# An attention kernel: one exponential over two PSUM banks, row maxima and projections on three shared banks

## The chip, the cores and the metric

The kernel runs on one core of a Trainium2 chip. The core's engines each work through their own list of instructions: TensorE (PE, matrix products into PSUM), VectorE (DVE), ScalarE (ACT, exponentials and copies), GpSimd (POOL) and SyncE (SP, which issues DMAs here). They wait for each other through semaphores. PSUM has eight banks of 128 partitions by 512 fp32 values. The metric is the device time of one execution in microseconds; the median of three runs counts.

## What is computed

Two attention layers run over 2,048 positions with 32 heads of 16 dimensions; their outputs are put side by side. Half A is softmax attention, half B a linear attention with softmax feature maps:

```python
# A
q, k, v = split(x @ wqkv)                       # 32 heads x 2048 x 16 each
p = softmax(einsum("bhqd,bhkd->bhqk", q, k) * 16 ** -0.5)
a = einsum("bhqk,bhkd->bhqd", p, v) merged @ wo
# B
pq, pk = q @ w_phi, k @ w_phi                   # per head, 16 x 16
phi = concat([softmax(p_), softmax(-p_)])       # for q and for k
o = (phi_q @ (phi_k.T @ v)) / (phi_q @ sum(phi_k) + 1e-6)
b = o merged @ wo
out = concat([a, b], axis=-1)                   # 2048 x 1024, bf16
```

Half A dominates: 32 x 2048 x 2048 scores are computed twice, once for the row maxima and once, transposed, for the exponentials.

## The kernel before

The program is planned in Python. `_Plan.op` appends an instruction to an engine's list and works out which semaphores it has to wait for from the tokens in `deps`. Each engine then runs its list strictly in the order in which the planner emitted it, so the order of emission is the schedule.

The work of half A is cut into 32 units. A unit `u` is a group `g` of four heads (their dimensions lie on partitions 0, 32, 64 and 96 of `QT` and `KT`) and a chunk `c` of 512 queries. The main loop (L916 on) counts slots `tau`; a unit has 32 slots (`NQ`), so there are 1,024 slots with maxima (`total_q1`).

In each slot the loop emits, in this order:

- `emit_m1(tau)`: the first product, two matmuls (L723), 128 queries by 512 keys for two of the four heads, each into a bank of its own. The heads alternate by slot (`half`), and with them the banks: 0 and 1, or 2 and 3. The matmuls wait for the reduction two slots back (`r1.get(q1 - 2)`). Each unit makes 64 such maxima tiles.
- `emit_m2` for two blocks of the unit that started 43 slots earlier (`LAG`): the second product (L771), 128 keys by 512 queries, scores transposed, with the row maxima subtracted through two extra rows of `QT`. It uses the other two heads' row quarters than the first product of the same slot. Its banks come from a free list, `ring_free`, which starts as banks 4, 5 and 6.
- `emit_exp` for each of the two blocks: one ACT instruction (L782) per bank, into a slot of the 16-deep buffer `pT`. The bank goes back to the free list.
- calls that fall due in this slot (`later`): POOL, ACT and DVE steps of half B (among them two DVE reductions into `mB`, L462 and L464), and the normalisation of a finished unit.
- every second slot `emit_pv`: four matmuls (L796) that sum P.V over keys into bank 7.
- `bg_step`: one piece of a background job, four matmuls as a rule (projections, half B's products, output projection). A job takes the first bank of the free list and gives it back when ACT has been told to copy it out. In 237 slots the trace has a piece of a job; two kinds hold their bank over several slots (half B's key-value products for four, the output projection for two).
- `emit_fill`: matmuls on zeros (L823), so that each slot has at least two groups of four (`NCOL`) beside the two products. They go into bank 7 while P.V is open, or else into the first free bank.
- `emit_r1(tau)`: one DVE reduction (L735) over the two banks of the first product, into `part`.

When a unit's 64 maxima are there, `emit_mchain` reduces `part` to `mrow` (L744), POOL splits the values into two bf16 parts, and DMAs on SP put them into `QT`. After the last unit, `emit_last` normalises it and finishes the output projection of the last four tiles: `emit_acc` has summed seven of the eight groups before (28 matmuls, L874), three tiles early into banks 1 to 3 and one at the end.

The parts that carry the order around the change:

```python
deps = [qt_ready[(g, c)], kt_ready[(g, kc)], r1.get(q1 - 2)]   # emit_m1
bank = ring_free.pop(0)                                        # emit_m2
ring_free.append(bank)                                         # emit_exp
running.append([list(j[2]), j[3], bank, bank_reader.get(bank), j[4]])   # bg_step: a job starts
ring_free.append(r[2])                                         # bg_step: after its last piece
```

Of the kernel before, what the change touches and what calls it, by code (L numbers as in the profile page):

```python
# [6 lines left out]
ALU = mybir.AluOpType  # L7
# [87 lines left out]
def bass_concat_heads__softmax_full_mha__linear_kernel_hedgehog__prompt_kernel(  # L95
# [24 lines left out]
    with contextlib.ExitStack() as es:  # L120
        block = es.enter_context(nc.Block())

        def sb(name, shape, dt):
            return es.enter_context(nc.sbuf_tensor(name, shape, dt))
# [37 lines left out]
        Yd = sb("Yd", [128, 2, 512], F32)  # L162
        lr = sb("lr", [32, 2, 64], F32)
        OA = sb("OA", [128, 2, 512], BF)
        part = sb("part", [128, 2, 4, 4, NKC], F32)
        mrow = sb("mrow", [128, 2, 16], F32)
        trow = sb("trow", [128, 2, 16], F32)
        BD = sb("BD", [128, 4, 128], BF)
# [95 lines left out]
        def later(slot, fn):  # L264
            calls.setdefault(slot, []).append(fn)
# [442 lines left out]
        def decode_q1(q1):  # L708
            u = q1 // NQ
            j = q1 % NQ  # L710
            if u == 0:
                return u, (j // 2) % 4, j // 8, j % 2
            return u, j // (2 * NKC), (j // 2) % NKC, j % 2

        def emit_m1(q1):
            u, qt, kc, half = decode_q1(q1)
            g, c = units[u]
            q0 = c * 512 + qt * 128
            deps = [qt_ready[(g, c)], kt_ready[(g, kc)], r1.get(q1 - 2)]
            tok = None  # L720
            for i in range(2):
                r = 2 * half + i
                tok = P.op("pe", lambda e, r=r: e.matmul(  # L723
                    PS[:, r, :], QT[32 * r:32 * r + 32, g, q0:q0 + 128],
                    KT[32 * r:32 * r + 32, g, kc * 512:(kc + 1) * 512],
                    start=True, stop=True, tile_position=(32 * r, 0)), deps, signal=(i == 1))
                deps = []
            m1[q1] = tok

        def emit_r1(q1):  # L730
            u, qt, kc, half = decode_q1(q1)
            deps = [m1[q1]]
            if q1 % NQ == 0 and u >= 2:
                deps.append(rm_t[u - 2])
            r1[q1] = P.op("dve", lambda e: e.tensor_reduce(  # L735
                part[:, u % 2, 2 * half:2 * half + 2, qt, kc], PS[:, 2 * half:2 * half + 2, :],
                AX.X, ALU.max), deps)

        def emit_mchain(u):
            ub = u % 2  # L740
            deps = [r1[q] for q in range(u * NQ, (u + 1) * NQ)]
            if u >= 2:
                deps.append(lo_t[u - 2])
            rm_t[u] = P.op("dve", lambda e: e.tensor_reduce(  # L744
                mrow[:, ub, :], part[:, ub].rearrange("p a b c -> p (a b) c"), AX.X, ALU.max), deps)
            hi_v = stage[:, ub, 0:16]
            lo_v = stage[:, ub, 16:32]
            hi = P.op("pool", lambda e: e.tensor_scalar(hi_v, mrow[:, ub, :], -1.0, None, ALU.mult),  # L748
                      [rm_t[u], t_stage0, mt_t.get(u - 2)])
            tt = P.op("pool", lambda e: e.tensor_tensor(trow[:, ub, :], mrow[:, ub, :], hi_v, ALU.add), [hi])  # L750
            lo_t[u] = P.op("pool", lambda e: e.tensor_scalar(lo_v, trow[:, ub, :], -1.0, None, ALU.mult), [tt])
            g, c = units[u]
            mt_t[u] = P.dma("sp", d_mt[ub], lambda e: e.dma_start_transpose(mcols[:, ub, :], stage[:, ub, :]),
                            [lo_t[u], mr_t.get(u - 2)])
            for hl in range(2):
                mr_t[u] = P.dma("sp", d_mr[ub], lambda e, hl=hl: e.dma_start(
                    QT[16 + hl:128:32, g, c * 512:(c + 1) * 512], mcols[16 * hl:16 * hl + 16, ub, :]), [mt_t[u]])
# [8 lines left out]
        def emit_m2(B):  # L766
            u, kt, r = block_info(B)
            g, c = units[u]
            bank = ring_free.pop(0)
            bank_of[B] = bank  # L770
            m2_t[B] = P.op("pe", lambda e: e.matmul(  # L771
                PS[:, bank, :], KT[32 * r:32 * r + 32, g, kt * 128:(kt + 1) * 128],
                QT[32 * r:32 * r + 32, g, c * 512:(c + 1) * 512],
                start=True, stop=True, tile_position=(32 * r, 0)),
                [bank_reader.get(bank), mr_t[u], kt_ready[(g, kt // 4)]])
            if B % 2 == 1:
                last_m2[u] = m2_t[B]

        def emit_exp(B):
            slot = B % RING  # L780
            bank = bank_of[B]
            exp_t[B] = P.op("act", lambda e: e.activation(  # L782
                pT[:, slot, :], PS[:, bank, :], ACT.Exp, scale=0.25), [m2_t[B], slot_reader.get(slot)])
            bank_reader[bank] = exp_t[B]
            ring_free.append(bank)

        def emit_pv(u, kt):
            g, c = units[u]
            Bs = [u * NB + 4 * kt + j for j in range(4)]
            deps = [exp_t[B] for B in Bs] + [vp_ready[kt], t_vp1]  # L790
            if kt == 0 and u >= 1:
                deps.append(xev_t[u - 1])
            tok = None
            for B in Bs:
                r = block_info(B)[2]
                tok = P.op("pe", lambda e, B=B, r=r: e.matmul(  # L796
                    PVB[32 * r:32 * r + 17, :], VP[:, kt, 4 * g + r, :], pT[:, B % RING, :],
                    start=(kt == 0), stop=(kt == NKT - 1), tile_position=(0, 32 * r)),
                    deps, signal=(B == Bs[-1]))
                deps = []  # L800
            if u == NU - 1:
                for B in Bs:
                    r = block_info(B)[2]
                    tok = P.op("pe", lambda e, B=B, r=r: e.matmul(  # L804
                        PS[32 * r:32 * r + 32, 0, :], ones_t[:, 0:32], pT[:, B % RING, :],
                        start=(kt == 0), stop=(kt == NKT - 1), tile_position=(0, 32 * r)),
                        [r1[total_q1 - 2]] if kt == 0 else [], signal=(B == Bs[-1]))
            for B in Bs:
                slot_reader[B % RING] = tok
            pv_t[(u, kt)] = tok  # L810
            pv_open[0] = (kt != NKT - 1)

        def emit_fill(ngroups):
            if pv_open[0]:
                bank, dep = 7, None
            elif ring_free:
                bank = ring_free[0]
                dep = bank_reader.get(bank)
            else:
                return  # L820
            for d in range(ngroups):
                for cq in range(4):
                    P.op("pe", lambda e, cq=cq: e.matmul(  # L823
                        PS[32 * cq:32 * cq + 17, bank, :], ones_t[:, 0:17], zmv[:, :],
                        start=(bank != 7), stop=(bank != 7), tile_position=(0, 32 * cq)),
                        [t_zmv, t_ones, dep] if (d == 0 and cq == 0) else [], signal=False)
# [26 lines left out]
        def emit_mul(u, tau):  # L853
            g, c = units[u]
            ub = u % 2
            for half in range(2):
                sl = slice(256 * half, 256 * half + 256)
                lo = c * 512 + 256 * half
                mul_t[u] = P.op("pool", lambda e, sl=sl, lo=lo: e.tensor_tensor(  # L859
                    QT[:, g, lo:lo + 256], X[:, ub, sl], Yd[:, ub, sl], ALU.mult),  # L860
                    [sh_t[u], xev_t[u], last_m2[u]])
            if g == NG - 2 and c == NQC - 1:
                for k in range(3):
                    later(tau + 4 + 2 * k, lambda k=k: emit_acc(k, k + 1, [mul_t[u], r1[total_q1 - 1], t_wo]))
            if g == NG - 1:
                for k in range(4):
                    add_job(tau + 4 + 4 * k, *oproj_job(4 * c + k))
# [11 lines left out]
        def emit_last():  # L879
            u = NU - 1  # L880
            g, c = units[u]
            done = pv_t[(u, NKT - 1)]
            bank = ring_free.pop(0)
            emit_acc(3, bank, [bank_reader.get(bank)])
            ln, ex, ml = {}, {}, {}
            for half in range(2):
                sl = slice(256 * half, 256 * half + 256)
                ln[half] = P.op("act", lambda e, sl=sl: e.activation(Yd[:, 1, sl], PS[:, 0, sl], ACT.Ln),
                                [done, mul_t[u - 2]])
            for half in range(2):  # L890
                sl = slice(256 * half, 256 * half + 256)
# [24 lines left out]
        while tau <= max(pv_in_slot) or jobs or running or calls:  # L916
# [3 lines left out]
            blocks = [2 * Pg, 2 * Pg + 1] if 0 <= Pg < total_q1 else []  # L920
            for B in blocks:
                emit_m2(B)
            for B in blocks:
                emit_exp(B)
            for fn in calls.pop(tau, []):
                fn()
            ncol = 0
# [12 lines left out]
            ncol += bg_step(tau)  # L940
            if ncol < NCOL:
                emit_fill(NCOL - ncol)
            if tau < total_q1:
                emit_r1(tau)
            for u in rm_in_slot.get(tau, []):
                emit_mchain(u)
            tau += 1
# [55 lines left out]
```

## Time and profile before

| | |
|---|---|
| timed runs | 1344.26, 1341.41, 1335.71 us; median 1341.41 |
| profiled execution, its own time (span) | 3156.6 us; no other time is recorded for it |
| DVE busy | 1304.1 us, of which L735 1255.2 (1,024 x 1.226) |
| ACT busy | 1296.2 us, of which L782 1111.5 (2,048 exponentials) |
| POOL busy | 307.0 us |
| PE busy | 3152.2 us in 12,226 matmuls |
| granted TensorE clock | 1.000 throughout |

The profiled execution is one run under the hardware profiler. A busy time is the sum over an engine's instructions, overlaps counted once; a group's line gives source line, engine, operation, what is written from what, the shapes and the count, then busy time and the mean length of one instruction, then the engine's idle time just before them and what ended it. In the timeline the first number is the start in us, the second the length of the merged row, `x8` the number of instructions in it, and the square bracket the idle time before it and what ended it. Matmul ends in it are modelled; the distance from one start to the next is the safer reading. The profiled execution took more than twice as long as the timed runs.

### The profile page before, as it was taken

The numbers are of one execution on the slowest core, as the hardware profiler recorded it, in microseconds if no ns is written. First come the engines' busy times: TensorE is split into PE (matmuls) and PEld (weight loads), VectorE is DVE, ScalarE is ACT, GpSimd is POOL, SyncE is SP. The second block draws the span as 40 slices with busy tenths as digits, with TensorE's granted clock in tenths as the row PEclk, the third lists the DMA queues.
The fourth block names the chain that finished last, engine by engine and source line by source line (L and its number), as shares of the span: only waits on it lengthen the run. The fifth ranks groups of instructions, "written<-read, shape, count | busy, mean of one in ns | idle before, by whom it ended". The sixth has DMA issues, their size and how long they took to land.

```text
span 3156.6 us, 29062 instructions
## 1 busy us (share of the span) xinstructions
PE 3152.2 (100%) x12226; PEld 362.2 (11%) x12226; DVE 1304.1 (41%) x1130; ACT 1296.2 (41%) x2479; POOL 307.0 (10%) x423
## 2 busy tenths in 40 slices
PE   9999999999999999999999999999999999999999
PEld 1111001111111111110011111111111111111111
DVE  1222223444444544544454435444454444445410
ACT  0001223444444444444444435444444444444442
POOL 1000000000011111111111101111111111111100
DMA  2000001000000000000000000000000000100000
GB/s 53 0 0 24 0 11 18 8 2 3 2 2 3 3 6 6 3 3 3 3 3 3 3 8 7 11 11 10 13 10 11 10 16 11 13 10 10 11 5 7
DMA packets 68939, 26.66 MB, mean 8 GB/s; under 512 B 59656, under 2 KB 66824, under 8 KB 68808
## 3 DMA queue, kind: packets, MB, share of 16 engines
q1 hardware_dynamic: 67464, 23.49, 5.4%
q8 instruction: 96, 1.57, 0.2%
q10 hardware_dynamic: 1344, 1.31, 0.1%
q14 instruction: 35, 0.29, 0.0%
HBM read 3.16 MB, written 4.19 MB: 2 GB/s over the span
## 4 chain that ended last, share of the span: by engine, by line
PE 99%; issue 0%; ACT 0%; POOL 0%; DVE 0%; POOLq 0%
PE PS L823 35%; PE PS L723 28%; PE PS L796 11%; PE PS L333 8%; PE PS L452 3%; PE PS L321 3%; PE PS L661 3%; PE PS L528 2%; PE PS L634 2%; PE PS L771 2%; PE PS L369 1%; PE PS L874 1%; PE PS L804 1%; PE PS L589 0%; PE PS L541 0%
## 5 line engine op out<-in xcount | busy, mean ns | idle before, releaser
L735 DVE TENSOR_REDUCE part<-PS 128x2 f32<-128x1024 f32 x1024 | 1255.2, 1226 | 1676.9 <-PE PS L723 1007.5
L782 ACT ACTIVATE pT<-PS 128x512 bf16<-128x512 f32 x2048 | 1111.5, 594 | 1262.1 <-PE PS L771 663.9
L823 PE MATMUL PS<-zmv,ones_t 128*17 128x512 bf16 x5004 | 1217.8, 973 | 0.3 <-ACT pT L782 0.3
L723 PE MATMUL PS<-KT,QT 32*128 32x512 bf16 x2048 | 959.5, 931 | 0.8 <-DVE QT L341 0.8
L771 PE MATMUL PS<-QT,KT 32*128 32x512 bf16 x2048 | 932.2, 902 | 0.0
L796 PE MATMUL PS<-pT,VP 128*17 128x512 bf16 x2048 | 457.2, 782 | 0.0
L723 PEld LDWEIGHTS PS<-KT,QT 32*128 32x128 bf16 x2048 | 111.0, 101 | 1580.8 <-DVE part L735 1102.9
L333 PE MATMUL PS<-xAT,WKp 128*128 128x512 bf16 x128 | 151.8, 1446 | 0.0
L823 PEld LDWEIGHTS PS<-zmv,ones_t 128*17 128x17 bf16 x5004 | 88.9, 88 | 315.1 <-issue 298.6
L771 PEld LDWEIGHTS PS<-QT,KT 32*128 32x128 bf16 x2048 | 111.1, 101 | 64.9 <-ACT pT L782 51.5
L333 PE MATMUL PS<-xAT,WQp 128*128 128x512 bf16 x128 | 116.5, 1122 | 0.0
L748 POOL TENSOR_SCALAR stage<-mrow 128x16 bf16<-128x16 f32 x32 | 8.1, 253 | 1070.4 <-DVE mrow L744 1070.4
L452 PE MATMUL PS<-WKp,xBT 128*128 128x512 bf16 x128 | 106.8, 1051 | 0.0
L345 ACT ACTIVATE KT<-PS,bias_k 128x512 bf16<-128x512 f32 x32 | 22.0, 687 | 194.9 <-PE PS L333 194.9
L507 POOL TENSOR_TENSOR wA<-eB,rB 128x1024 bf16<-128x1024 bf16 x32 | 61.7, 1929 | 398.1 <-ACT rB L501 398.1
L796 PEld LDWEIGHTS PS<-pT,VP 128*17 128x17 bf16 x2048 | 49.6, 87 | 378.0 <-issue 356.3
L321 PE MATMUL PS<-wA,xAT 128*128 128x512 bf16 x64 | 84.3, 1598 | 0.0
L859 POOL TENSOR_TENSOR QT<-X,Yd 128x256 bf16<-128x256 f32 x62 | 43.6, 725 | 400.6 <-DMA Yd<-Yd 400.4
L661 PE MATMUL PS<-WOp,QT 128*128 128x512 bf16 x96 | 80.8, 1063 | 0.0
L486 POOL TENSOR_TENSOR sB<-eB 128x512 f32<-128x512 bf16 x32 | 36.9, 1154 | 374.5 <-ACT eB L479 374.5
L471 POOL TENSOR_TENSOR uB<-pB,mB 128x512 f32<-128x512 f32 x32 | 33.9, 1058 | 395.9 <-DVE mB L462 395.9
L309 ACT ACTIVATE QT<-PS 128x512 bf16<-128x512 f32 x31 | 18.5, 597 | 93.7 <-PE PS L333 93.7
(78 smaller groups left out, 713.8 us busy)
## 6 DMA issues: line engine op xcount, KB each, us to landing
Yd<-Yd SPq DMA_DIRECT2D x124, 32.0 KB, 3.2
out_dram<-xAT SPq DMA_DIRECT2D x16, 128.0 KB, 1.7
out_dram<-OA SPq DMA_DIRECT2D x12, 128.0 KB, 1.7
wA<-in_A_wqkv_dram ACTq DMA_DIRECT2D x2, 512.0 KB, 5.0
QT<-mcols SPq DMA_DIRECT2D x64, 4.0 KB
wA<-in_A_wqkv_dram SPq DMA_DIRECT2D x1, 512.0 KB, 4.3
WOp<-in_A_wo_dram SPq DMA_DIRECT2D x4, 128.0 KB, 4.4
BD<-in_B_w_phi_dram SPq DMA_DIRECT2D x32, 0.5 KB, 1.6
```

Source lines behind the costliest of these rows:

```text
L321: piece = mm_piece(4, lambda e, b, ct: e.matmul(PS[:, b, :], xAT[:, ct, kt * 128:(kt + 1) * 128], wA[:, ct, 1024:1536], start=(ct == 0), s ...
L333: piece = mm_piece(4, lambda e, b, ct: e.matmul(PS[:, b, :], wpad[:, ct, g, :], xAT[:, ct, c * 512:(c + 1) * 512], start=(ct == 0), stop=( ...
L452: add_job(slot, [mm_piece(4, lambda e, b, ct: e.matmul(PS[:, b, :], xBT[:, ct, st * 128:(st + 1) * 128], Wf[:, x, ct, :], start=(ct == 0), ...
L528: piece = mm_piece(4, lambda e, b, ct: e.matmul(PS[:, b, :], xBT[:, ct, st * 128:(st + 1) * 128], wA[:, ct, 0:512], start=(ct == 0), stop= ...
L634: piece = mm_piece(4, lambda e, b, t: e.matmul(PS[:, b, :], oTB[:, i, t, :], woB[:, t, :], start=(t == 0), stop=(t == 3)), lambda: [cx["ot ...
L661: return mm_piece(4, lambda e, b, i: e.matmul(PS[:, b, :], QT[:, 4 * p + i, st * 128:(st + 1) * 128], WOp[:, 4 * p + i, :], start=(p == 0 ...
L723: tok = P.op("pe", lambda e, r=r: e.matmul(PS[:, r, :], QT[32 * r:32 * r + 32, g, q0:q0 + 128], KT[32 * r:32 * r + 32, g, kc * 512:(kc + 1 ...
L735: r1[q1] = P.op("dve", lambda e: e.tensor_reduce(part[:, u % 2, 2 * half:2 * half + 2, qt, kc], PS[:, 2 * half:2 * half + 2, :], AX.X, ALU ...
L771: m2_t[B] = P.op("pe", lambda e: e.matmul(PS[:, bank, :], KT[32 * r:32 * r + 32, g, kt * 128:(kt + 1) * 128], QT[32 * r:32 * r + 32, g, c ...
L782: exp_t[B] = P.op("act", lambda e: e.activation(pT[:, slot, :], PS[:, bank, :], ACT.Exp, scale=0.25), [m2_t[B], slot_reader.get(slot)])
L796: tok = P.op("pe", lambda e, B=B, r=r: e.matmul(PVB[32 * r:32 * r + 17, :], VP[:, kt, 4 * g + r, :], pT[:, B % RING, :], start=(kt == 0), ...
L823: P.op("pe", lambda e, cq=cq: e.matmul(PS[32 * cq:32 * cq + 17, bank, :], ones_t[:, 0:17], zmv[:, :], start=(bank != 7), stop=(bank != 7), ...
```

## The change

The banks are dealt out anew. The exponentials get banks 0 to 3 as two fixed pairs (`bank = B % 4`); one ACT instruction covers both banks of a slot and writes two neighbouring slots of `pT`. The first product takes its banks one by one from the free list of banks 4, 5 and 6, which it now shares with the background jobs.

A maximum is held until it can be reduced together with the next one. `emit_m1` reduces what is held when it has two neighbouring banks, when the next bank does not follow the held one, when a job holds a bank over several slots (`running`), when the reduction before was one over two banks (`single`), when the free list is empty, or at the end of a unit. So two-bank and one-bank reductions alternate where nothing intervenes. `part` becomes a flat list of 64 maxima per unit in order of issue, and `emit_mchain` reads it through a rearranged view. Each first-product matmul now waits for the last reader of its own bank and signals by itself.

At the end, the denominators of the last unit are summed in bank 4 instead of 0, two tiles of the output projection are summed early (banks 5 and 6) and two at the end (banks 0 and 1). Fill matmuls outside an open P.V are left out while a maximum is held.

```diff
-        part = sb("part", [128, 2, 4, 4, NKC], F32)
+        part = sb("part", [128, 2, 64], F32)
...
+        def emit_r1():
+            n, banks = held[0][0], [x[1] for x in held]
+            u, m = n // 64, n % 64
...
+            tok = P.op("dve", lambda e: e.tensor_reduce(
+                part[:, u % 2, m:m + len(banks)], PS[:, banks[0]:banks[0] + len(banks), :], AX.X, ALU.max), deps)
+            for x in held:
+                r1[x[0]] = tok
+                bank_reader[x[1]] = tok
+                ring_free.append(x[1])
+            single[0] = len(held) == 2
+            held.clear()
...
             for i in range(2):
                 r = 2 * half + i
+                n = 2 * q1 + i
+                bank = ring_free.pop(0)
+                if held and bank != held[0][1] + 1:
+                    emit_r1()
...
+                    [qt_ready[(g, c)], kt_ready[(g, kc)], bank_reader.get(bank)])
+                held.append((n, bank, tok))
+                if len(held) == 2 or running or single[0] or not ring_free or n % 64 == 63:
+                    emit_r1()
...
         def emit_m2(B):
-            bank = ring_free.pop(0)
-            bank_of[B] = bank
+            bank = B % 4
...
         def emit_exp(B):
             slot = B % RING
-            bank = bank_of[B]
-            exp_t[B] = P.op("act", lambda e: e.activation(
-                pT[:, slot, :], PS[:, bank, :], ACT.Exp, scale=0.25), [m2_t[B], slot_reader.get(slot)])
-            bank_reader[bank] = exp_t[B]
-            ring_free.append(bank)
+            bank = B % 4
+            exp_t[B] = exp_t[B + 1] = P.op("act", lambda e: e.activation(
+                pT[:, slot:slot + 2, :], PS[:, bank:bank + 2, :], ACT.Exp, scale=0.25),
+                [m2_t[B], m2_t[B + 1], slot_reader.get(slot), slot_reader.get(slot + 1)])
+            bank_reader[bank] = bank_reader[bank + 1] = exp_t[B]
...
-            elif ring_free:
+            elif ring_free and not held:
...
-                for k in range(3):
-                    later(tau + 4 + 2 * k, lambda k=k: emit_acc(k, k + 1, [mul_t[u], r1[total_q1 - 1], t_wo]))
+                for k in range(2):
+                    later(tau + 4 + 2 * k, lambda k=k: emit_acc(k, k + 5, [mul_t[u], bank_reader[k + 5], t_wo]))
...
-            bank = ring_free.pop(0)
-            emit_acc(3, bank, [bank_reader.get(bank)])
+            for k in (2, 3):
+                emit_acc(k, k - 2, [bank_reader[0], t_wo])
```

## The prediction

> **What bounds it now.** I read the page's busy times first, then its costliest groups, then a stretch of the timeline from the middle of the run.
>
> ```profile
> span 3156.6 us, 29062 instructions
> PE 3152.2 (100%) x12226; PEld 362.2 (11%) x12226; DVE 1304.1 (41%) x1130; ACT 1296.2 (41%) x2479; POOL 307.0 (10%) x423
> L735 DVE TENSOR_REDUCE part<-PS 128x2 f32<-128x1024 f32 x1024 | 1255.2, 1226 | 1676.9 <-PE PS L723 1007.5
> L782 ACT ACTIVATE pT<-PS 128x512 bf16<-128x512 f32 x2048 | 1111.5, 594 | 1262.1 <-PE PS L771 663.9
> L823 PE MATMUL PS<-zmv,ones_t 128*17 128x512 bf16 x5004 | 1217.8, 973 | 0.3 <-ACT pT L782 0.3
> ```
>
> The first line is the trap of this profile. The profiled execution took 3156.6 us and the timed runs 1341.41 us (median), so the profile is not a slow copy of the run to be predicted. In the profile TensorE is busy all the time and sets the pace. In the timed runs the same list of matmuls must have gone at least 2.35 times faster. DVE and ACT durations do not depend on TensorE's speed, and their sums, 1304.1 and 1296.2 us, are 97% of 1341. So the profiled execution gives the durations of DVE and ACT and the order of the work, and I set up the sum as a difference that is added to the timed median, not to the span.
>
> ```profile
> 1003.88 0.91 PE L723 MATMUL PS<-KT,QT 32*128 32x512 bf16 x2
> 1003.89 0.90 PE L771 MATMUL PS<-QT,KT 32*128 32x512 bf16 x2
> 1004.72 1.75 PE L823 MATMUL PS<-zmv,ones_t 128*17 128x512 bf16 x8
> 1004.83 1.23 DVE L735 TENSOR_REDUCE part<-PS 128x2 f32<-128x1024 f32 x1 [1.14 <-PE PS L771]
> 1004.86 1.08 ACT L782 ACTIVATE pT<-PS 128x512 bf16<-128x512 f32 x2 [1.27 <-PE PS L771]
> 1006.40 0.91 PE L723 MATMUL PS<-KT,QT 32*128 32x512 bf16 x2
> ```
>
> This is one slot. The four matmuls of the two products start within 0.01 us and share one pass of 0.84 us (1003.88 to 1004.72). Two more passes follow (eight fills, or four P.V matmuls and four fills), and at 1006.40 the next slot begins: a slot is three passes, in program order. DVE starts 0.11 us after the pass ends. ACT's two exponentials take 1.08 us together, so the second starts 0.49 us after the first.
>
> ```profile
> 399.66 1.23 DVE L735 TENSOR_REDUCE part<-PS 128x2 f32<-128x1024 f32 x1 [2.61 <-PE PS L771]
> 400.80 0.21 DVE L744 TENSOR_REDUCE mrow<-part 128x16 f32<-128x64 f32 x1
> 401.09 0.25 POOL L748 TENSOR_SCALAR stage<-mrow 128x16 bf16<-128x16 f32 x1 [160.61 <-DVE mrow L744]
> ```
>
> A waiting DVE instruction starts 1.14 us after a reduction of 1.226: 0.086 overlaps. The reader on POOL starts 0.08 us after DVE's end (401.01 to 401.09); I take that for TensorE too.
>
> DVE at its own pace therefore needs 1024 x 1.14 = 1167 us, plus 38 for the 64 reductions into mB (676 ns each, 0.59 start to start) and 4 for mrow: 1209 us. ACT needs 1024 x 0.98 = 1004 plus about 160 for its other 185 busy us: some 1165. DVE is the bound of the timed run, ACT close behind. The remaining 1341 - 1209 = 132 us are the start, the 43 slots after the last maximum, and losses; with some 60 for the first two, about 70 are losses.
>
> **The exponential.** From 272 to 512 elements a PSUM copy on ACT goes from 400 to 597 ns, 0.82 ns an element; 1024 elements then cost 594 + 420 = 1.01 us, and the SBUF exponential of that size (L479, 1.056) is the other end. Less 0.10 overlap, a slot's exponentials drop from 0.98 to about 0.92. That is 60 us of ACT, hidden behind DVE; only the last 43 slots, without maxima, keep it: -2 us. The extra wait (for both second products and two pT slots) has nothing late behind it, since four banks hold two slots' worth.
>
> **The maxima, by count.** The free list decides which are paired, and it is bookkeeping: I followed it through 2,048 maxima with the background jobs in the slots where the trace has them (237 slots). Undisturbed, it alternates two, one, two, one. A job takes a bank and turns the list; where its order becomes 6, 5, 4 no two neighbours follow each other, and only singles are made until another job turns it back. The count is 482 pairs and 1,084 singles. A pair costs 1.14. A single is not in the trace: 0.593 is the start-to-start row of a 512-element reduction from SBUF (mB), 0.692 the full duration of a 512-element PSUM copy on DVE (L341). I take 0.692 - 0.086 = 0.606, because it reads PSUM. DVE: 482 x 1.14 + 1084 x 0.606 = 1206 against 1167, **+39 us** (+25 at 0.593, +133 at 0.692). All of it lies on the bound.
>
> [...]
>
> **The maxima, by order.** Here is the larger cost. Two maxima are issued per slot, and three banks go round. In undisturbed alternation, slot A writes banks 4 and 5 (pair Pa), slot B writes 6 (single) and 4, and slot C writes 5 and 6. The second matmul of slot B must wait for the end of Pa, which reads bank 4. It stands at the head of TensorE's queue: behind it are the slot's second products, P.V, job and fill, and behind those the partner of its pair, the first matmul of slot C. Let p be the time of a pass and Pa start at 0. Pa ends at 1.226; the matmul starts at 1.31; three passes later the partner starts, one pass later it is done, and DVE sees it at 1.42 + 4p. DVE was free at 1.14 + 0.606 = 1.75. It idles 4p - 0.33 us. Before the change nothing like it happens: while DVE reduces one pair, the other pair of banks is already free, and TensorE has a whole 1.14 us for three passes. Singles do not starve either: with three banks a matmul waits for the third reduction back.
>
> p in the timed runs is in no trace. The profile's passes (full-width matmuls of L874 start 0.56 us apart at the least, mostly 0.84) are too slow to be it. From above: all passes must fit into 1341.4 us. There are 1,067 of the two products, 512 of P.V, 5004/4 = 1,251 of fill, 672 of full-width job matmuls and some 110 others, 3,612, so p is at most 0.371. From below only zero. The nearest row is the ceiling, and it holds only if TensorE never waited, while DVE and ACT are loaded to some 90%. I take two thirds of it, 0.25: DVE idles 0.67 us.
>
> Of the 482 pairs, 231 straddle two slots; in the others both matmuls are in one slot and come 0.08 + p + 0.11 after the pair before, within the single's 0.606. So **231 x 0.67 = +155 us** (0 at p below 0.08; 231 x 1.15 = +267 at 0.371). A reduction into mB can fall into such a gap, -15 us for 32 x 1.19 at two chances in five.
>
> [...]
>
> **Small terms.** In the first 38 or so slots a job runs in each, and maxima and job share three banks: a pair's bank is held p + 0.11 + 1.226 + 0.08 = 1.67 us, a single's 1.13, a job's 4p + 0.88 = 1.88, about 4.7 us per slot over three banks, 1.56 per slot against five passes (1.25) before: +12 us. At the end 14 accumulating matmuls instead of 7 stand before the last four, partly beside the Ln, Exp and multiply: +2. Fills are left out where a maximum is held, at unit boundaries: nothing, DVE is the bound. [...]
>
> Sum: 1341 - 2 + 39 + 155 - 15 + 12 + 2 = **1532 us**.
>
> **Rivals.** (1) *The gap does not open, and the ring relaxes.* The exponentials get four banks of their own, and a slot with a job no longer leaves the second products two. If the 70 us of losses come from that, the time is 1341 + 39 - 70 = 1310. For it: ACT and DVE are both near their limits and had three banks between exponentials and jobs. Against it: it needs the gap below (70 - 39)/231 = 0.13 us, p below 0.115, a third of the ceiling. Chance 0.09 for faster by over 1% (such a difference is about what can be told from none), 0.05 for a balance within 1%. (2) *TensorE is nearly the bound as well*, p from 0.33 to 0.371: the gap is 1.0 to 1.15, the term 229 to 267, the time 1605 to 1645 and, with jobs that no longer fit under DVE, up to 1660. For it: passes at the ceiling explain 1341 without any loss. Chance 0.12. (3) *The list does not alternate as I followed it*: if jobs fall otherwise and it stays in singles, DVE needs 2048 x 0.606 = 1241, +74, without a gap: 1415. Chance 0.04. The forecast, p from 0.14 to 0.33 (1430 to 1605), has 0.70.
>
> **The numbers.** The range 1410 to 1640 takes in the forecast, (3) and half of (2). Faster 0.09, same 0.05, slower 0.86.
>
> **What would show it.** The changed profile should have 482 two-bank reductions at 1.23 us and 1,084 one-bank ones near 0.69, and 1,024 exponentials near 1.02. If it is again paced by TensorE at 0.84 a pass, it will not show the gap: the waiting matmul comes 1.67 us after the pass, Pa ends 1.34 after it. Its span then stays within 3080 to 3200 while the timed runs get slower. If TensorE runs at full pace in it, DVE should idle some 0.67 us ahead of each straddling pair, and the first product's matmuls should wait for the reduction. The prediction fails if passes are so short that order costs nothing, if singles are far from 0.606, or if DVE does not set the time.

## The result and the profile after

The changed kernel takes 1741.26 us (median of 1748.6, 1741.6, 1740.91 and 1728.95) against 1340.68 us before, a ratio of 1.298 with a 95% interval of 1.292 to 1.304. The forecast was 1532 us, 1410 to 1640. The direction held, the size did not: 400 us were lost where 191 had been summed.

This time TensorE ran at its real pace under the profiler. The kernel before was therefore profiled again, also at that pace (experiment e0), and everything below is compared with that profile, whose span of 1341.5 us answers to the timed runs. Page of the changed kernel: span, busy times, TensorE's granted clock by fortieths of the span, and the exponential's group.

```profile
span 1746.7 us, 28076 instructions
PE 1408.9 (81%) x11978; PEld 338.9 (19%) x11978; DVE 1300.5 (74%) x1672; ACT 1199.3 (69%) x1455; POOL 307.4 (18%) x423
PEclk7558998799888997999889888888887999878889
L796 ACT ACTIVATE pT<-PS 128x1024 bf16<-128x1024 f32 x1024 | 1028.0, 1024 | 376.9 <-PE PS L785 369.7
```

The same rows of the kernel before, from e0 (the last is from its groups by shape):

```profile
span 1341.5 us, 29062 instructions
PE 1208.0 (90%) x12226; PEld 343.3 (26%) x12226; DVE 1224.7 (91%) x1130; ACT 1214.3 (91%) x2479; POOL 307.4 (23%) x423
PEclk9999999999999999997999989999899999999999
L735 DVE TENSOR_REDUCE part<-PS 128x2 f32<-128x1024 f32 x1024 | 1180.2, 1216 | 58.2 <-PE PS L771 53.4 <-PE PS L723 0.5
```

Groups by shape of the changed kernel, DVE's maxima: busy, mean ns, then DVE's idle time ahead of them.

```profile
L724 DVE TENSOR_REDUCE part<-PS 128x1 f32<-128x512 f32 x1084 | 706.4, 683 | 143.4 <-PE PS L785 77.2 <-PE PS L743 63.4
L724 DVE TENSOR_REDUCE part<-PS 128x2 f32<-128x1024 f32 x482 | 590.2, 1224 | 247.7 <-PE PS L785 189.3 <-PE PS L743 54.3
```

These rows hold the whole loss. DVE was busy with maxima for 1180.2 us and idle ahead of them for 58.2; now it is 1296.6 in the two rows, 1253.2 with overlaps counted once (the page's row for the line), and 391.1 idle. That is 73 + 333 = 406 us, against 405 us between the spans. ACT did get lighter (1214.3 to 1199.3 busy), but it went from 91% to 69% loaded: it waits. And the granted clock, 0.981 in the mean of e0, is 0.853.

The straddling pair is to be seen in the timeline. TensorE, changed kernel, full clock, no job near:

```profile
815.67 0.39 PE L743 MATMUL PS<-KT,QT 32*128 32x512 bf16 x1
816.54 0.38 PE L743 MATMUL PS<-KT,QT 32*128 32x512 bf16 x1 [0.49 <-DVE part L724]
816.54 0.39 PE L785 MATMUL PS<-QT,KT 32*128 32x512 bf16 x2
816.86 0.39 PE L810 MATMUL PS<-pT,VP 128*17 128x512 bf16 x4
817.08 0.39 PE L840 MATMUL PS<-zmv,ones_t 128*17 128x512 bf16 x4
817.40 0.39 PE L743 MATMUL PS<-KT,QT 32*128 32x512 bf16 x2
```

and DVE over the same stretch (x4: two, one, two and one bank, back to back):

```profile
813.51 3.56 DVE L724 TENSOR_REDUCE part<-PS 128x2 f32<-128x1024 f32 x4 [0.75 <-PE PS L785]
817.82 1.82 DVE L724 TENSOR_REDUCE part<-PS 128x2 f32<-128x1024 f32 x2 [0.75 <-PE PS L785]
```

The matmul at 816.54 waited for the pair that ended at 816.47 (third of the four: 813.51 + 1.13 + 0.60, and 1.226 long). Behind it came the second products, P.V and fill, and only at 817.40 its partner; DVE, done at 817.07, starts at 817.82. One such gap in every 4.31 us, three slots. Before (e0), DVE's row for the same time has six reductions over two banks each and no gap:

```profile
809.67 6.87 DVE L735 TENSOR_REDUCE part<-PS 128x2 f32<-128x1024 f32 x6
```

All time can be laid out by slots (starts of the first product; "near a job": a matmul of a job in the slot or in the one before; the first 43 slots, when no exponentials run yet, apart). Half clock is the time at which 0.5 was granted; where a slot is called one at full clock, 1.0 was granted at its start.

| kernel | span, us | half clock, us | first 43 slots, us | 648 slots without a job, us each | 331 near a job, us each | DVE idle ahead of maxima, us |
|---|---|---|---|---|---|---|
| before (e0) | 1341.5 | 54 | 51.6 | 1.164 | 1.408 | 58 |
| after | 1746.7 | 514 | 107.5 | 1.464 | 1.885 | 391 |
| e1 partners side by side | 1644.3 | 479 | 104.9 | 1.342 | 1.810 | 297 |
| e2 singles | 1464.3 | 155 | 68.9 | 1.224 | 1.618 | 106 |
| e5 singles, jobs apart | 1405.0 | 113 | 54.1 | 1.260 | 1.407 | 51 |
| e11 side by side, jobs apart | 1429.6 | 90 | 59.1 | 1.239 | 1.505 | 106 |

From the first two rows: 648 x 0.300 = 194 us in slots without a job, 331 x 0.477 = 158 near jobs, 56 at the start.

The start differs in one thing more. A fill outside an open P.V is left out while a maximum is held, and in the first 43 slots P.V is never open: 16 fill matmuls are left there of 72, and half clock was granted for 92 of the 107 us (the fives in the changed kernel's row of the clock), against none in e0. In e2, e5 and e11 all 72 are back, and half clock is gone from these slots.

### The profile page after: what moved, and what is told of

Its sections match the earlier page's. It is cut to its first block, busy times and chain, and to the rows that moved or that the text cites. A ratio compares the mean times of both kernels' runs of the same rounds, so it can differ in the third digit from the quotient of the medians.

```text
span 1746.7 us, 28076 instructions
## 1 busy us (share of the span) xinstructions
PE 1408.9 (81%) x11978; PEld 338.9 (19%) x11978; DVE 1300.5 (74%) x1672; ACT 1199.3 (69%) x1455; POOL 307.4 (18%) x423
## 4 chain that ended last, share of the span: by engine, by line
PE 46%; DVE 41%; ACT 10%; issue 1%; DMA 1%; POOL 0%; SPq 0%; ACTq 0%; POOLq 0%
DVE part L724 39%; PE PS L743 18%; PE PS L840 9%; ACT pT L796 6%; PE PS L810 5%; PE PS L333 4%; PE PS L785 2%; PE PS L321 2%; PE PS L661 1%; PE PS L528 1%; PE PS L452 1%; PE PS L634 1%; DVE mB L464 1%; DVE mB L462 1%; ACT KT L345 1%
## 5 line engine op out<-in xcount | busy, mean ns | idle before, releaser
L724 DVE TENSOR_REDUCE part<-PS 128x1 f32<-128x512 f32 (+1 forms) x1566 | 1253.2, 850 | 391.1 <-PE PS L785 266.5
L796 ACT ACTIVATE pT<-PS 128x1024 bf16<-128x1024 f32 x1024 | 1028.0, 1024 | 376.9 <-PE PS L785 369.7
L743 PE MATMUL PS<-KT,QT 32*128 32x512 bf16 x2048 | 636.8, 436 | 237.2 <-DVE part L724 194.6
L840 PE MATMUL PS<-zmv,ones_t 128*17 128x512 bf16 x4756 | 449.6, 426 | 12.1 <-DVE part L724 12.1
L785 PE MATMUL PS<-QT,KT 32*128 32x512 bf16 x2048 | 442.7, 429 | 0.1
L810 PE MATMUL PS<-pT,VP 128*17 128x512 bf16 x2048 | 223.5, 427 | 13.6 <-ACT X L309 13.3
L333 PE MATMUL PS<-xAT,WKp 128*128 128x512 bf16 x128 | 46.3, 500 | 8.0 <-DVE part L724 6.6
L333 PE MATMUL PS<-xAT,WQp 128*128 128x512 bf16 x128 | 42.9, 469 | 7.5 <-DVE part L724 7.1
L452 PE MATMUL PS<-WKp,xBT 128*128 128x512 bf16 x128 | 38.6, 430 | 10.5 <-DVE part L724 9.7
L661 PE MATMUL PS<-WOp,QT 128*128 128x512 bf16 x96 | 26.5, 401 | 11.1 <-DVE part L724 11.0
```

Of the source, the lines that this page charges most:

```text
L333: piece = mm_piece(4, lambda e, b, ct: e.matmul(PS[:, b, :], wpad[:, ct, g, :], xAT[:, ct, c * 512:(c + 1) * 512], start=(ct == 0), stop=( ...
L452: add_job(slot, [mm_piece(4, lambda e, b, ct: e.matmul(PS[:, b, :], xBT[:, ct, st * 128:(st + 1) * 128], Wf[:, x, ct, :], start=(ct == 0), ...
L661: return mm_piece(4, lambda e, b, i: e.matmul(PS[:, b, :], QT[:, 4 * p + i, st * 128:(st + 1) * 128], WOp[:, 4 * p + i, :], start=(p == 0 ...
L724: tok = P.op("dve", lambda e: e.tensor_reduce(part[:, u % 2, m:m + len(banks)], PS[:, banks[0]:banks[0] + len(banks), :], AX.X, ALU.max), ...
L743: tok = P.op("pe", lambda e, r=r, bank=bank: e.matmul(PS[:, bank, :], QT[32 * r:32 * r + 32, g, q0:q0 + 128], KT[32 * r:32 * r + 32, g, kc ...
L785: m2_t[B] = P.op("pe", lambda e: e.matmul(PS[:, bank, :], KT[32 * r:32 * r + 32, g, kt * 128:(kt + 1) * 128], QT[32 * r:32 * r + 32, g, c ...
```

## The experiments

Four theories stood against each other: ORDER (a maximum's matmul waits at the head of TensorE's list, and its partner stands three passes behind it), JOBS (a job takes one of three banks), CLOCK (waiting TensorE loses its clock), COUNT (more DVE instructions). In the edits below, `...` stands for lines left out, and the comments are added here.

### e0: the kernel before, at TensorE's real pace

No edit.

> The kernel before the change, unchanged, for a profile in which TensorE runs as fast as in the timed runs. Its span should be near 1340 us. Theory ORDER AND JOBS (the time after the change is lost where a first-product matmul waits for a bank: straddling pairs, 190 us of DVE idle, and slots near a job, 180 us): here DVE should idle only some 70 to 80 us ahead of its maxima, nearly all of it near jobs, and slots without a job should take 1.14 to 1.18 us at whatever clock is granted. Theory CLOCK (the change's waits let TensorE idle, the granted clock halves, and longer passes make the loss): here the granted clock should be above 0.95 in the middle of the run, against 0.86 after the change. If the clock here is as low as after the change, it isn't the clock that costs the 400 us.

Measured: 1343.24 us, clock 0.981. A slot without a job takes 1.159 us at full clock, and counted from start to start DVE idles 76 us, 58 of it near jobs from slot 43 on. The 70 us of losses that the prediction had inferred were there, and near jobs.

### e1: partners side by side

```diff
+            if late_m1:
+                held[0] = held[0][:2] + (late_m1.pop()(),)
...
+                alone = not (held or running or single[0] or not ring_free or n % 64 == 63)
+                if i == 1 and alone:        # would be held at the end of the slot
+                    late_m1.append(mm)
+                    held.append((n, bank, None))
+                    continue
```

> After the change, but a maximum's matmul that would be held alone at the end of its slot is emitted at the start of the next slot, right ahead of its partner. Banks, pairs and singles stay the same (482 and 1,084), only the place of 231 matmuls in TensorE's list moves. Theory ORDER: the partner no longer has three passes in front of it, so the 190 us of DVE idle ahead of straddling pairs fall to below 40 and the time to about 1550 to 1600; what is lost near jobs (180 us) stays. Theory CLOCK: some more comes back as TensorE waits less. Theory BANKS (three banks are too few however the matmuls are ordered): the wait is only moved, the time stays above 1700.

Measured: 1638.08 us (ratio 1.220, 1.213 to 1.228). By shape:

```profile
L724 DVE TENSOR_REDUCE part<-PS 128x1 f32<-128x512 f32 x1084 | 709.0, 683 | 194.1 <-PE PS L794 136.2 <-PE PS L747 55.5
L724 DVE TENSOR_REDUCE part<-PS 128x2 f32<-128x1024 f32 x482 | 589.6, 1223 | 102.4 <-PE PS L794 52.4 <-PE PS L747 47.5
```

The idle time ahead of pairs fell from 247.7 to 102.4 us. For straddling pairs, at full clock and without a job near, it went from a mean of 0.75 to 0.07 us, so ORDER is right about that gap. BANKS falls as the main cause, but a part of the wait did move: the idle time ahead of singles rose by 51, most of it at half clock away from jobs (12 to 49 us), and the clock stayed at 0.855. So 103 us came back instead of the 140 to 190 expected.

### e2: every maximum by itself

```diff
-                if len(held) == 2 or running or single[0] or not ring_free or n % 64 == 63:
-                    emit_r1()
+                emit_r1()
```

> After the change, but every maximum is reduced by itself: 2,048 one-bank reductions. DVE's own work grows from 1206 to about 2048 x 0.60 = 1229 us. Theory ORDER: no pair straddles two slots, 190 us of idle vanish and 23 are added: about 1570, less if the clock recovers. Theory COUNT (more and smaller DVE instructions are what costs): 1741 + 23 or more, slower than after the change.

Measured: 1463.4 us (ratio 1.090, 1.087 to 1.094), 278 us less than after the change although DVE has 482 instructions more. Groups and clock:

```profile
PEclk9999999999999989998999899989899999999999
L724 DVE TENSOR_REDUCE part<-PS 128x1 f32<-128x512 f32 x2048 | 1255.8, 681 | 106.1 <-PE PS L784 59.3
```

COUNT falls as the main cause. A bank is given back after 0.68 us instead of 1.22, a matmul waits for the third reduction back, and no partner is needed. Half clock falls from 514 to 155 us. Slots near jobs gained as well (1.885 to 1.618 us each), and so did the first 43 (107.5 to 68.9 us), which the expectation had not counted. No maximum is ever held here, so 240 of the 248 fill matmuls that the change leaves out are back; this run doesn't part that from the rest.

### e3: two exponentials per slot again

```diff
+            for k in range(2):
+                exp_t[B + k] = P.op("act", lambda e, k=k: e.activation(
+                    pT[:, slot + k, :], PS[:, bank + k, :], ACT.Exp, scale=0.25),
+                    [m2_t[B + k], slot_reader.get(slot + k)])
...
```

> After the change, but the two banks of a slot are exponentiated by two ACT instructions, as before the change. ACT's work grows by about 0.06 us in each of 1,024 slots, some 55 us in all. Theory DVE AND TENSORE (ACT isn't on the path in the 1,024 slots with maxima): the time stays within 10 us of 1741, or falls a little because a second product's bank comes free earlier. Rival ACT (the one wide exponential is what holds up the second products, or ACT is still the bound): 30 us or more in either direction.

Measured: 1750.09 us, ratio 1.302 (1.297 to 1.308), which overlaps that of the change itself (1.292 to 1.304). ACT's busy time rose from 1199.3 to 1256.8 us and nothing followed. What the change saves on ACT is not on the path in the changed kernel.

### e4: fill where TensorE waits

```diff
+                if wide_reader.pop(bank, False):     # the bank is being read by a pair
+                    emit_ahead(q1, 2 - i)            # that many groups of four fills
...
```

> After the change, with fill matmuls added where TensorE would wait anyway: two groups of four ahead of a slot's first maximum, one ahead of its second, if that matmul has to wait for a two-bank reduction. The order of all other work stays. Theory CLOCK (waits leave TensorE idle, the granted clock halves for 514 of 1747 us, passes are longer in them; by the slots' lengths at full and at half clock that costs some 60 us in the 981 slots from slot 43 on and 30 in the first 43): the clock rises above 0.95 and the time falls by 60 to 90 us, to 1650 to 1680. Rival (the low clock is only a sign of the waits and costs nothing by itself): the clock rises, the time stays within 20 us of 1741. A slot without a job at full clock should stay at 1.41 us in both.

Measured: 1746.42 us (1735.43, 1757.41). The clock only rose to 0.89, half clock fell from 514 to 383 us, and the slots without a job kept their 1.464 us: at full clock they had become longer by the fills (1.425 against 1.410). In the first 43 slots, where it adds 72 fills, half clock fell from 92 to 34 us and their time from 107 to 91. Over the whole run it neither shows nor excludes a price of the clock.

### e5: singles, with the jobs on other banks

```diff
-        ring_free = [4, 5, 6]
+        ring_free = [0, 1, 2, 3]                     # jobs and exponentials, one bank each
+        max_free = [4, 5, 6]                         # maxima alone
...
```

> The version with every maximum reduced by itself (1463 us), but the jobs take their banks from 0 to 3, shared with the exponentials, which are one instruction per bank again; the maxima have banks 4 to 6 to themselves. Theory JOBS (a job takes one of the maxima's three banks, and DVE idles near it: 104 us from slot 43 on, 92 us for the first 43 slots up from 52): idle near jobs falls to about the 58 us of the kernel before, the first 43 slots lose 15, the time falls to 1390 to 1410. Rival LONG SLOTS (a job's four passes make its slot long whoever owns the bank): within 15 us of 1463.

Measured: 1407.45 us (ratio 1.049, 1.045 to 1.054). JOBS is shown: with the same DVE work and the same fills as e2, slots near a job fall from 1.618 to 1.407 us, to what the kernel before has (1.408), the first 43 from 68.9 to 54.1; slots without a job are a little longer (1.224 to 1.260). LONG SLOTS falls. The exponentials are one per bank here, which by e3 makes no difference in the changed kernel.

```profile
L725 DVE TENSOR_REDUCE part<-PS 128x1 f32<-128x512 f32 x2048 | 1250.3, 682 | 50.5 <-PE PS L786 46.4
```

The row also closes the account. Idle time is no longer than before the change (50.5 against 58.2); what is left of the loss, 63.5 us between the spans, is DVE's 1250.3 - 1180.2 = 70 us of additional work.

### e6 and e7: a fill group less, a fill group more

```diff
-    NCOL = 2
+    NCOL = 1        # e6; 3 in e7
```

> After the change with one group of fills per slot less (P.V or one fill instead of two groups). Theory ORDER: the partner of a straddling pair has two passes in front of it instead of three, each gap is 0.27 us shorter, a slot without a job at full clock takes 1.32 instead of 1.41 us; with the clock unchanged that is 231 x 0.27 = 62 us less, 1680. Theory CLOCK: TensorE idles more, the clock falls below 0.80 and eats the gain, 1741 or more.

> After the change with one group of fills per slot more. Theory ORDER: four passes in front of the partner, each gap 0.27 us longer, a slot without a job at full clock 1.50 us; with the clock unchanged 62 us more, 1800. Theory CLOCK: the clock rises above 0.95, which gives 60 to 90 us back: 1710 to 1740.

Measured: 1893.06 us at a clock of 0.571 and 1743.49 at 0.947, one execution each. From the start of the waiting matmul to its partner's it takes 0.649, 0.865 and 1.080 us with one, two and three groups (medians at full clock without jobs, in e6 of seven pairs only), so a pass of fill adds 0.215 us, and the gap grows with the passes as ORDER says; its median goes 0.62, 0.83, 1.05. The fractions of the clock for e6 and then e7:

```profile
PEclk7566555565655755555555665555555575555557
```

```profile
PEclk7679999999999999998999998999899999999999
```

With fewer passes the order costs less, and the whole run is slower all the same, by 152 us: CLOCK is real too. With more, slots without a job get longer (1.464 to 1.492 us) and those near jobs shorter (1.885 to 1.815), and the sum stays.

### e8: side by side, one fill group more

The edits of e1 and e7 together.

> The version with the partners side by side (1638 us, granted clock 0.855), with one group of fills per slot more. The extra pass lies off DVE's path here, since the partner no longer has the passes in front of it. Theory CLOCK: the clock rises above 0.94, the slots without a job fall from a mean of 1.34 to about 1.24 us, and 60 to 120 us come back: 1520 to 1580. Rival (a low clock costs nothing where DVE sets the pace): above 1610.

Measured: 1653.33 us (ratio 1.231, 1.224 to 1.238), no better than e1's 1638. The clock rose to 0.951 as meant, but the expectation was wrong in holding the additional pass to be off DVE's path: slots without a job at full clock went from 1.237 to 1.354 us, probably because TensorE, with four passes a slot, arrives later at the pair. This does not isolate the clock either.

### e9 and e10: the kernel before with fewer and more fills

`NCOL = 1` and `NCOL = 3` in the kernel before.

> The kernel before the change with one group of fills per slot less, so that the clock can fall while order, banks and DVE's work stay. Theory CLOCK HAS ITS OWN PRICE: the clock falls below 0.8, DVE idles more than the 76 us it idles now, above all near jobs, and the time rises by 40 us or more. Theory CLOCK COSTS ONLY BEHIND A WAIT (before the change, maxima are two slots ahead of their banks' need): the clock falls, the time stays within 20 us of 1341.

> The kernel before the change with one group of fills per slot more. Its clock is at half for 54 of 1341 us, and DVE idles 25 us in those stretches. Theory CLOCK: they go, and 10 to 25 us come back, 1316 to 1331, faster than both kernels. Rival (TensorE's slot is then long enough to be late, four passes near 1.0 us and a job on top): 1341 or more.

Measured: 1407.53 us (one execution) at a clock of 0.792, and 1381.04 (ratio 1.028, 1.024 to 1.033) at 0.996. e9 prices the clock without the change: 587 us at half clock, about as many as after the change, cost 64 us, although there is a pass less per slot. DVE's idle time ahead of the maxima rises from 58.2 to 104.0 us:

```profile
L735 DVE TENSOR_REDUCE part<-PS 128x2 f32<-128x1024 f32 x1024 | 1190.2, 1218 | 104.0 <-PE PS L771 97.8
```

e10 is a miss: half clock falls from 54 to 13 us, and the fourth pass costs more than that gives (at full clock 1.189 us a slot without jobs against 1.159, near jobs 1.445 against 1.393). No version tried beats the kernel before.

### e11: side by side, and jobs apart

The edits of e1 and e5 together, pairs kept: 672 pairs and 704 singles. The version also leaves no fill out while a maximum is held, and a running job no longer forces a single.

> The partners side by side, and the jobs on banks 0 to 3 with the exponentials, which are one instruction per bank: maxima alternate undisturbed over two banks and one, 682 pairs and 684 singles by the list. If ORDER, JOBS and the DVE count are all that the change costs, what is left is the count: 682 x 1.14 + 684 x 0.60 = 1188 us against 1167, and 1341 + 21 plus some 10 for the clock: 1360 to 1385. If something else costs (the third bank comes free too late whatever the order), it stays above 1420.

Measured: 1434.13 us (ratio 1.067, 1.061 to 1.074), above the expected 1385. With both repairs and the fills, 307 us of the 400 are gone, 204 of them between e1 and this version, but something remains:

```profile
L725 DVE TENSOR_REDUCE part<-PS 128x2 f32<-128x1024 f32 x672 | 822.1, 1223 | 87.4 <-PE PS L796 58.4 <-PE PS L748 25.0
L725 DVE TENSOR_REDUCE part<-PS 128x1 f32<-128x512 f32 x704 | 478.1, 682 | 18.8 <-PE PS L796 15.9
```

DVE's idle time is nearly all ahead of pairs. Straddling pairs near a job, at full clock, still have a mean of 0.35 us (131 of them), away from jobs 0.08. A likely reason, not tested, is that with a job's passes in the slot TensorE reaches the two matmuls late. Singles on three banks of their own (e5) bear the jobs better than alternating pairs (1.407 us a slot near a job against 1.505).

## Why the prediction was wrong

**The bound and the losses before**: right. DVE sets the pace; the 70 us of losses were 76 in e0.

**The exponential**: right, 1.024 us for 1.01, and hidden (e3).

**The maxima, by count**: right. 482 pairs and 1,084 singles, as followed through the free list. From the traces a pair is 1.131 and a single 0.597 us start to start (0.683 from start to end), so the term is 1192 - 1158 = 34 us for +39.

**The maxima, by order**: the mechanism is right (e1, e7), the size nearly. The prediction had 231 x 0.67 = 155 us; the straddling pairs have 190. Its chain was 0.08 + 4 x 0.25 + 0.11 us; it is 0.055 from the pair's end to the waiting matmul, 0.865 to its partner, 0.422 from there to DVE, 1.34 instead of 1.19. Most of the difference lies in the three passes, which are not alike: 0.32 from the two products to P.V, 0.22 from P.V to fill, 0.32 from fill to the next products, as the rows from 816.54 to 817.40 show, 0.288 in the mean where 0.25 was taken. The last step, 0.422 for p + 0.11 = 0.36, is the rest. With 0.288 the prediction's own 4p - 0.33 gives 0.82 us, and 231 of these are 190 (the measured 190 include pairs at half clock and near jobs, so that the two agree to the microsecond is chance). One fill after another adds 0.215 us (e6 and e7), less than the passes around the products: 0.215 for all of them would make the gap 4 x 0.215 - 0.33 = 0.53 us, further from the measured 0.83 than the forecast's 0.67.

**Where it failed: jobs were priced only for "the first 38 or so slots", at +12 us, and the clock not at all.** The sum starts from 1341 and so carries the 70 us of losses over unchanged; no term lets them grow near the jobs after the start, or in slower passes. Start to start DVE idles 444 us after the change (the clock is taken at the gap, so the sums differ by some us with the way of counting):

| DVE idle ahead of maxima, us | before (e0) | after |
|---|---|---|
| from slot 43, no job in the slot or the two before, full clock | 12 | 93 (86 of it straddling pairs) |
| the same, half clock | 2 | 53 |
| from slot 43, near jobs, full clock | 35 | 113 |
| the same, half clock | 23 | 126 |
| first 43 slots | 3 | 58 |

The first line is what the prediction reckoned with. The third is what it left out of its bank arithmetic, done for the first slots only: a bank that a job holds until ACT has copied it leaves the maxima two, in 237 slots all over the run. e5 shows that this is the bank and not the long slot. For the first 43 slots the arithmetic was not far off: e2, which shares the banks too but is at full clock there, is 17 us longer than e0 in them, where +12 was written. The other 39 of their 56 us came with half clock, and "Fills are left out where a maximum is held, at unit boundaries: nothing" overlooks these slots; in e4, 72 fills added there came with 16 us less. How the 39 divide between missing fills, pairs and clock no run shows.

The second and fourth lines are idle time at half clock. They are not the clock's price as a whole, since the same waits would cost something at full clock too, but the clock makes them longer (three passes take 1.51 us at half clock, 0.86 at full), and none of the rivals named it; the profile to be read from had a granted clock of 1.000 and no hint of a drop. Rival (2) had TensorE near its bound through passes of 0.33 us or more at a steady pace. The measured 0.288, and a gap of 0.83 us where it needed 1.0, exclude that.

How much of the 405 us is the clock's stays open. If all slots from 43 on had the mean length of those that began at full clock (1.410 and 1.820 us), the run would be 57 us shorter; by the slots without any half clock in them (1.381 and 1.700) it would be 117. With the first 43 slots at e2's 68.9 that makes about 95 to 155. Neither end is a bound, because long waits and half clock come together (in the windows of the last section TensorE streamed for 41% of the time ahead of half clock, for 58% ahead of full clock), and a slot's length does not tell how much is owed to which. At e9's price, 64 us for 533 us more of half clock, the 460 more here would be 55 us, an estimate from a kernel with a pass less per slot. Experiments e4, e7 and e8, meant to hold the clock up, changed the slots too.

**The mB reductions in the gaps** (-15): at most half. Only 16 straddling pairs stand right behind an instruction other than a maximum, with a mean gap of 0.37 instead of 0.86: 8 us. **The end** (-2, +2): from the last maximum on, 52.5 us against 56.3.

**What the profile would show**: the counts and lengths came as written. That it would again be paced by a slow TensorE did not; it showed the gap, 0.83 us start to start where 0.67 was written.

## What to carry to other kernels

When buffers are dealt out anew, follow the shared free list through the whole run for every user of it, the rare ones too: here a job in every fourth slot, on the smaller pool, cost nearly as much as the steady pattern (158 us near jobs, 194 away from them, both with the clock's part). A wait that is put at the head of an in-order list is priced by everything between it and the work that the bound engine needs next, up to the arrival of the result there, so a matmul's 0.42 us belongs in the sum and not its pass alone, and passes of different kinds are priced apart, 0.32 and 0.22 us here. And if waits are added to an engine whose granted clock goes with its load, as here (0.981 before the change, 0.853 after it), the clock needs a term of its own: in e9, 533 us more of half clock came with 64 us.

## What the runs showed of the hardware

The granted clock falls without a long pause. In the changed kernel the longest time without a matmul from slot 43 on is 1.7 us, and yet 0.5 was granted for 514 us, in stretches that are multiples of 3.4 us; its trace has no other value than 1.0 and 0.5. Cut into windows of that length, some 300 windows at full clock that were followed by another at full clock had TensorE streaming for 58% of the time on average (a pass of 512 columns counted as 0.215 us, a pass of fill in e6 and e7); some 50 that were followed by half clock had 41%, none above 50%. In e0 the same means are 68% and 35%, in e9 63% and 44%. So the share within a window goes with the clock. A sharp limit does not come out: windows that kept full clock go down to 40% (e9), windows that lost it up to 61%.

At half clock a slot's three passes take 0.54, 0.39 and 0.57 us in the changed kernel (medians), 1.51 together against 0.86 at full clock. In e0 the seven slots without a job that lie wholly in half clock take 1.51 us each, against 1.159 at full clock: TensorE sets the pace there, not DVE.

The first profile of the kernel before, at 2.35 times the timed runs' length, was an outlier of TensorE alone: by kind of neighbours its passes have medians of 0.54 to 1.11 us, against 0.22 to 0.32 in e0 at full clock, and yet its granted clock is given as 1.000, with no change of clock in the trace. The maxima took 1.226 us each there and 1.216 in e0, the exponentials 0.594 and 0.601.
